# Fused attention and two MLPs on one core: raw weights of the key stage in batch 0's buffers, first attention ahead of a step's narrowing, last weight splits two blocks apart

## The chip, the cores and the metric

The kernel runs on one core of a Trainium2 chip. The metric is the device time of one execution in microseconds (us), as the median of three runs. The engines are called PE (TensorE, matrix multiplication), DVE (VectorE), ACT (ScalarE) and POOL (GpSimd); SP issues the DMAs.

## The reference

The weights of the two MLPs arrive as float64; the kernel reads them as pairs of 32-bit integers ("wide" weights) and makes float32 of them itself, which is called narrowing here. The reference, cut to what matters:

```python
def sm_attn(qq, kk, vv):                  # softmax attention, scale 1/sqrt(64)
    ...
p_packed = sm_attn(p, k, v)               # 32 packed rows per head read k and v
out = sm_attn(q, p_packed, p_packed)      # 576 rows per head read the packed rows
x = out.transpose(0, 2, 1, 3).reshape(4608, 512)      # 8 batches x 576 rows, 8 heads x 64
xn = x / sqrt(mean(x * x) + 1e-6) * rms_g
x = (silu(xn @ w_gate) * (xn @ w_val)) @ w_out        # 512 -> 1536 -> 512
h = x @ moe2_w_in                                     # 512 -> 2048
return (h * cos(h)) @ moe2_w_out                      # 2048 -> 512
```

## The kernel before

A float32 product is made of three matmuls (`mm3`, L151 to L153): each operand is split into a high and a low part (`hilo`, high on ACT, L101, low on DVE or POOL, L102).

**Key stage** (about the first 178 us). Its loop runs over 18 steps; step i deals with one pair of batch and half of the heads, 16 pairs in all. A step loads one or two raw weights (`w_load`, 512 KB each, 20 over the stage: 16 of w_gate and w_val, 4 of w_out), loads K for step i+4, stores finished tiles, then does on PE the transposes of the previous exponentials (`u_et`, tile et), its own scores (`u_s1`, L391, 16 matmuls into s) and the transposes of the next K (`u_prep`, `u_kt`, tiles pt and kp); DVE takes the maximum over the scores (L395, mx), ACT the exponential. Then `u_pp` multiplies with V into pp (result cd on DVE, L433). Between these stand other pieces of work:

- Narrowing of the raw weight that was loaded one step before: part a on ACT (L129), part b on DVE, four operations (L137, L140, L143, L146) that end in the tile wy or, for w_out, ny. A w_out weight is split besides (wohl).
- Attention of batch 0 (`attend(0)`), cut into parts by the words of `ATT_ORD0`; `bg0_step(i, n)` takes the next n parts. x parts multiply, ACT squares and DVE adds into ssq (L295); r sums ssq on PE (rp, L301) and DVE makes ri of it (L303); s scales the attention rows by it (L312); p transposes them (atp) and splits the result (apt), which the projection reads. One part is taken ahead of `u_pp`, two more (one from step 15 on) at the end of the step. 34 parts belong to the key stage.
- `unit(0, u)`: the weights of batch 0, multiplied out on PE (mps) and split into wmhl.

The order is written by hand: each engine runs its instructions in the order of the code, and SP issues all DMAs in that order too. Raw weights lie in five places of the pool u3 (tag wraw).

**Projection stage**: 8 batches of 24 blocks; a block is 12 matmuls gv, silu (ACT L677, DVE L678 and L679), the split shl, and 12 matmuls acc. Its first steps in batch 0 load, narrow and split the weights that remain (wy 16 to 23, w_out 4 to 11; `wy_prep`, `WO_AT`) in a pool wo1 of eight places that is opened when the key stage is over.

**Last stage**: 144 blocks hp (12 matmuls), kk, r, |r|, sine and product (`h_block`, L876 to L883), and the output matmuls ops. Its first weights are read back in float32 (wmraw), and split (wmhl) on ACT and POOL by `wm_split`. A scheduler sets the order of this stage.

Of the kernel before, what the change touches and what calls it, by code (L numbers as in the profile page):

```python
# [20 lines left out]
def kernel(  # L21
# [14 lines left out]
    nc = tc.nc  # L36
# [39 lines left out]
    WO_AT = {4: (-1, 0), 5: (1, 3), 6: (3, 6), 7: (6, 9), 8: (9, 11), 9: (10, 13), 10: (13, 15), 11: (14, 17)}  # L76
# [103 lines left out]
    gT = u1.tile([128, H], F32, name="gT")  # L180
# [149 lines left out]
    def load_k(i):  # L330
# [3 lines left out]
        pn = u3.tile([128, 2, D], F32, tag="pn", name="pn", bufs=3)  # L334
# [23 lines left out]
    load_v(2)  # L358

    def u_prep(i):  # L360
# [4 lines left out]
        nc.vector.tensor_copy(pT[i % 2][:, :, :NP], pt.rearrange("p (h n) -> p h n", h=4))  # L365
        z["kT"], z["kn"] = u4.tile([128, 4, HALF], F32, tag="kT", name="kT"), kn
# [17 lines left out]
    def u_s1(i):  # L384
# [3 lines left out]
        pz = pT[i % 2].rearrange("p h x -> p (h x)")  # L388
# [160 lines left out]
    def wm_split(pool=wm_p):  # L549
# [27 lines left out]
    for i in range(NG + 2):  # L577
# [38 lines left out]
        load_v(i + 3)  # L616
        bg0_step(i, 0 if i == U_ATT else 2 if i < 15 else 1)
# [7 lines left out]
    wo_p = [wo_p[0], ctx.enter_context(tc.tile_pool(name="wo1", bufs=NF1 - WO_U, reuse_waits="tile"))]  # L625
# [225 lines left out]
    while wm_q:  # L851
        wm_split()
# [112 lines left out]
```

## Time and profile before

| | us |
|---|---|
| median of 3 runs | 1755.45 (1754.77 to 1756.66) |
| profiled execution | 1762.2 |
| its span in the profile | 1760.4 |
| PE busy in the span | 1685.1 (96%) |
| DVE busy | 1119.1 (64%) |
| ACT busy | 835.2 (47%) |
| POOL busy | 68.7 (4%) |
| DMA queue of SP | 163.62 MB, 30.5% of the span |

Times in the profile count from the start of the span. Steps of the key stage can be told by their first score matmul: step 0 begins at 8.75 us, step 7 at 71.21, step 8 at 82.73, step 10 at 103.59, step 13 at 132.08 and step 14 at 146.61; the first gv of the projection is at 177.60.

### The profile page before, as it was taken

The numbers are of one execution on the slowest core, as the hardware profiler recorded it, in microseconds if no ns is written. First come the engines' busy times: TensorE is split into PE (matmuls) and PEld (weight loads), VectorE is DVE, ScalarE is ACT, GpSimd is POOL, SyncE is SP. The second block draws the span as 40 slices with busy tenths as digits, with TensorE's granted clock in tenths as the row PEclk, the third lists the DMA queues.
The fourth block names the chain that finished last, engine by engine and source line by source line (L and its number), as shares of the span: only waits on it lengthen the run. The fifth ranks groups of instructions, "written<-read, shape, count | busy, mean of one in ns | idle before, by whom it ended". The sixth has DMA issues, their size and how long they took to land.

```text
span 1760.4 us, 28289 instructions
## 1 busy us (share of the span) xinstructions
PE 1685.1 (96%) x11184; PEld 1463.1 (83%) x11184; DVE 1119.1 (64%) x2180; ACT 835.2 (47%) x1597; POOL 68.7 (4%) x66
## 2 busy tenths in 40 slices
PE   6776889999999999999999999999999999999998
PEld 5554778999999898999999788888888888888887
DVE  2566787677777686866556755555555656565554
ACT  3454443444444444444445654555455545455453
POOL 0000321000000000000002100000000000000000
PEclk9888899999999999999999999999999999999999
DMA  9993732345352534442234200000000000000000
GB/s 232 263 249 117 225 134 94 125 145 182 110 194 92 179 121 161 137 138 76 86 104 139 86 22 27 24 25 24 25 24 25 24 25 25 25 1 25 0 25 24
DMA packets 90564, 165.42 MB, mean 94 GB/s; under 512 B 26432, under 2 KB 48960, under 8 KB 90432
## 3 DMA queue, kind: packets, MB, share of 16 engines
q1 hardware_dynamic: 90432, 163.62, 30.5%
q8 instruction: 88, 1.44, 0.3%
q14 instruction: 44, 0.36, 0.1%
HBM read 128.45 MB, written 35.13 MB: 93 GB/s over the span
## 4 chain that ended last, share of the span: by engine, by line
PE 83%; DVE 6%; DMA 6%; ACT 3%; issue 1%; SPq 0%; POOL 0%; DVEq 0%; ACTq 0%
PE ops L153 7%; PE ops L151 7%; PE ops L152 7%; PE hp L151 7%; PE hp L152 7%; PE hp L153 7%; PE gv L151 5%; PE acc L151 5%; PE acc L152 5%; PE acc L153 5%; PE gv L152 5%; PE gv L153 5%; PE mps L523 3%; PE sp L234 2%; DMA kn<-in_k_dram 1%; PE s L391 1%
## 5 line engine op out<-in xcount | busy, mean ns | idle before, releaser
L151 PE MATMUL gv<-apt,wmhl 128*128 128x288 f32 x768 | 237.8, 310 | 7.7 <-DVE silu L678 6.3
L151 PE MATMUL acc<-shl,wohl 128*128 128x288 f32 x768 | 235.3, 306 | 6.2 <-ACT x L711 5.7
L152 PE MATMUL acc<-shl,wohl 128*128 128x288 f32 x768 | 229.1, 298 | 0.0
L153 PE MATMUL acc<-shl,wohl 128*128 128x288 f32 x768 | 228.8, 298 | 0.0
L152 PE MATMUL gv<-apt,wmhl 128*128 128x288 f32 x768 | 227.6, 296 | 0.0
L151 PE MATMUL hp<-xhl,wmhl 128*128 128x512 f32 x576 | 224.8, 390 | 2.3 <-DVE r L883 2.3
L153 PE MATMUL gv<-apt,wmhl 128*128 128x288 f32 x768 | 226.7, 295 | 0.0
L152 PE MATMUL hp<-xhl,wmhl 128*128 128x512 f32 x576 | 224.8, 390 | 0.0
L153 PE MATMUL hp<-xhl,wmhl 128*128 128x512 f32 x576 | 224.7, 390 | 0.0
L151 PE MATMUL ops<-w2hl,ghl 128*128 128x512 f32 x576 | 224.2, 389 | 0.0
L152 PE MATMUL ops<-w2hl,ghl 128*128 128x512 f32 x576 | 224.1, 389 | 0.0
L153 PE MATMUL ops<-w2hl,ghl 128*128 128x512 f32 x576 | 222.7, 389 | 0.0
L883 DVE TENSOR_TENSOR r<-r,hp 128x512 f32<-128x512 f32 x144 | 99.1, 688 | 185.3 <-ACT r L882 185.3
L881 ACT ACTIVATE r<-r 128x512 f32<-128x512 f32 x144 | 91.1, 633 | 244.8 <-DVE r L880 244.7
L101 ACT ACTIVATE shl<-silu 128x288 fp32r<-128x288 f32 x192 | 85.4, 445 | 235.6 <-DVE silu L679 233.6
L151 PEld LDWEIGHTS gv<-apt,wmhl 128*128 128x128 f32 x768 | 145.0, 189 | 50.0 <-DVE silu L678 9.6
L876 ACT ACTIVATE kk<-hp,magic 128x512 f32<-128x512 f32 x144 | 99.3, 690 | 125.3 <-PE hp L153 125.2
L151 PEld LDWEIGHTS acc<-shl,wohl 128*128 128x128 f32 x768 | 145.8, 190 | 6.8 <-ACT x L711 6.0
L152 PEld LDWEIGHTS acc<-shl,wohl 128*128 128x128 f32 x768 | 146.1, 190 | 0.0
L152 PEld LDWEIGHTS gv<-apt,wmhl 128*128 128x128 f32 x768 | 145.5, 189 | 0.0
L153 PEld LDWEIGHTS acc<-shl,wohl 128*128 128x128 f32 x768 | 145.4, 189 | 0.0
L153 PEld LDWEIGHTS gv<-apt,wmhl 128*128 128x128 f32 x768 | 145.2, 189 | 0.0
(131 smaller groups left out, 2965.6 us busy)
## 6 DMA issues: line engine op xcount, KB each, us to landing
wy<-wy SPq DMA_DIRECT2D x96, 512.0 KB, 4.3
kn<-in_k_dram SPq DMA_DIRECT2D x16, 576.0 KB, 6.5
vn<-in_v_dram SPq DMA_DIRECT2D x48, 192.0 KB, 5.8
qnat<-in_q_dram SPq DMA_DIRECT2D x32, 288.0 KB, 5.1
x_dram<-x SPq DMA_DIRECT2D x32, 288.0 KB, 2.8
x1raw<-x_dram SPq DMA_DIRECT2D x18, 512.0 KB, 4.0
raw<-in_moe_w_in_dram SPq DMA_DIRECT2D x16, 512.0 KB, 5.8
raw<-in_moe_w_out_dram SPq DMA_DIRECT2D x16, 512.0 KB, 5.2
```

Of the source, the lines that this page charges most:

```text
L101: nc.scalar.activation(out=hi, in_=src, func=AF.Copy)
L151: nc.tensor.matmul(ps, lhi, rhi, start=first, stop=False)
L152: nc.tensor.matmul(ps, lhi, rlo, start=False, stop=False)
L153: nc.tensor.matmul(ps, llo, rhi, start=False, stop=last)
L234: nc.tensor.matmul(sp[:, i, 2 * c:2 * c + 2, :], qT[:, i, c * CP:(c + 1) * CP], bq[:, 2 * j + i], start=True, stop=True,)
L391: nc.tensor.matmul(s1[:, r, :HALF], pz[rows, h * 128:(h + 1) * 128], kT[rows, h], start=h == 0, stop=h == 3)
L523: nc.tensor.matmul(ps[kt][h * NP:(h + 1) * NP], ppT[b // 4][rows, 4 * kt + h, n:n + NP], w_y[2 * u + kt][rows, j], start=True, stop=True,)
L876: nc.scalar.activation(out=kk, in_=hp, func=AF.Identity, scale=1.0 / TWO_PI, bias=magic[:, 0:1])
L881: nc.scalar.activation(out=r, in_=r, func=AF.Abs)
L883: nc.vector.tensor_tensor(out=r, in0=r, in1=hp, op=ALU.mult)
```

## The change

1. The pool wo1 is opened ahead of the key stage, and the stage's raw weights use its eight places (tag wo; in the order they read as wo where they read wraw before). The pools u3 and u4 go; V has three places instead of four, pn four instead of three, pT one tile instead of two.
2. The 20 raw weights come in steps 1 to 15 instead of 1 to 16, two at steps 3, 6, 9, 12 and 15 (before: 4, 8, 12 and 16). Two weights are so narrowed in steps 4, 7, 10, 13 and 16 (before: 5, 9, 13 and 17).
3. Four raw weights of batch 0 (wy 16, 17, 18 and w_out 4) are loaded in steps 15 to 17 (`B0_L`); the rest is loaded three ahead instead of two, and w_out 4 is narrowed one block later.
4. V is loaded at the end of step i for step i+2 instead of i+3, and one V load ahead of the stage goes.
5. The second call of `bg0_step` stands ahead of part b of the narrowing and always takes two parts, so the 34th is taken in step 16 and not in step 17.
6. In the passage to the last stage two weight items are split on DVE instead of POOL, at blocks 3 and 5, the next two are loaded there, and the loads and splits of the next x rows come two blocks (the second split one block) later.

```diff
-    WRAW_B = 5
...
-    W_FROM, W_TO = 1, 17
+    W_FROM, W_TO = 1, 16
...
+    B0_L = {15: (16,), 16: (17, -4), 17: (18,)}
...
-    WO_AT = {4: (-1, 0), 5: (1, 3), 6: (3, 6), 7: (6, 9), 8: (9, 11), 9: (10, 13), 10: (13, 15), 11: (14, 17)}
+    WO_AT = {4: (-1, 1), 5: (0, 3), 6: (3, 6), 7: (6, 9), 8: (9, 11), 9: (10, 13), 10: (13, 15), 11: (14, 17)}
...
-    wo_p = [ctx.enter_context(tc.tile_pool(name="wo0", bufs=WO_U))]
+    wo_p = [ctx.enter_context(tc.tile_pool(name=f"wo{x}", bufs=(WO_U, NF1 - WO_U)[x])) for x in range(2)]
...
-    u3 = ust.enter_context(tc.tile_pool(name="u3", bufs=2))
-    u4 = ust.enter_context(tc.tile_pool(name="u4", bufs=1))
-    u5 = ust.enter_context(tc.tile_pool(name="u5", bufs=2))
...
-    pT = [u1.tile([128, 4, 160], F32, name=f"pT{i}") for i in range(2)]
-    for t in pT:
-        nc.gpsimd.memset(t, 0.0)
+    pT = u1.tile([128, 4, 160], F32, name="pT")
+    nc.gpsimd.memset(pT, 0.0)
...
-        pn = u3.tile([128, 2, D], F32, tag="pn", name="pn", bufs=3)
+        pn = u2.tile([128, 2, D], F32, tag="pn", name="pn", bufs=4)
...
-        vn = nat_v[i] = u2.tile([CP, 4, NC_, D], F32, tag="vn", name="vn", bufs=4)
+        vn = nat_v[i] = u2.tile([CP, 4, NC_, D], F32, tag="vn", name="vn", bufs=3)
...
-    load_v(2)
...
-        w_raw[n] = load_w(pool, tag, w[r:r + 128, c * 512:(c + 1) * 512], bufs, kt == 1)
+        w_raw[n] = load_w(wo_p[1], "wo", w[r:r + 128, c * 512:(c + 1) * 512], swap=kt == 1)
...
-        wo_raw[f] = load_w(pool, tag, w_out[f * 128:(f + 1) * 128, :], {"wraw": WRAW_B}.get(tag))
+        wo_raw[f] = load_w(wo_p[1], "wo", w_out[f * 128:(f + 1) * 128, :])
...
-    def wm_split(pool=wm_p):
+    def wm_split(pool=wm_p, eng=None):
...
-            hilo(raw[:, :, a * 128:(a + 1) * 128], t[:, 0], t[:, 1], (nc.vector, nc.gpsimd)[pool is wm_p])
+            hilo(raw[:, :, a * 128:(a + 1) * 128], t[:, 0], t[:, 1], eng or nc.gpsimd)
...
         load_k(i + 4)
+        for n in B0_L.get(i, ()):
+            (wy_load if n >= 0 else wo_load)(abs(n))
...
             unit(0, U_S[i])
+        bg0_step(i, 0 if i == U_ATT else 2)
         for n in w_q:
             w_prep(n, 1)
         for n in wo_q:
             wo_split(n - W_KV, 1)
         wo_q = [n for n in w_q if n >= W_KV]
         w_q = due
-        load_v(i + 3)
-        bg0_step(i, 0 if i == U_ATT else 2 if i < 15 else 1)
+        load_v(i + 2)
...
-    wo_p = [wo_p[0], ctx.enter_context(tc.tile_pool(name="wo1", bufs=NF1 - WO_U, reuse_waits="tile"))]
...
-    for n in range(W_B0, W_B0 + 2):
-        wy_load(n, wo_p[1], "wo")
-    wo_load(WO_U, wo_p[1], "wo")
     for _ in bg0:
         pass
     att_load(1)
...
-            if n + 2 < 4 * NCK:
-                wy_load(n + 2, wo_p[1], "wo")
+            if n + 3 < 4 * NCK:
+                wy_load(n + 3)
...
-    while wm_q:
-        wm_split()
...
+            late_x = 2 * (n == 0)
+            if f == 10 + late_x and n + 1 < NCH:
                 load_x(n + 1)
-            if f in (12, 14) and n + 1 < NCH:
-                split_x(n + 1, f // 14)
-            if n == 0 and f in (3, 4):
-                wm_load(("w", NCK + f - 3))
-            if n == 0 and f in (9, 11):
-                wm_split(b4)
+            if f in (12 + late_x, 14 + late_x // 2) and n + 1 < NCH:
+                split_x(n + 1, f // (14 + late_x // 2))
+            if n == 0 and f in (3, 5, 9, 11):
+                wm_split(wm_p if f < 6 else b4, nc.vector)
+            if n == 0 and f in (3, 5):
+                wm_load(("w", NCK + f // 4))
```

What becomes of the order, at three places. DVE in step 13 of the key stage, before (from the last squares of batch 0's attention, ssq, to ri):

```order
L295 TENSOR_TENSOR ssq<-ssq,sq 128x288
L433 TENSOR_SCALAR cd<-pp,mx 128x128
L137 TENSOR_SCALAR wy<-wy 128x512
L140 TENSOR_SCALAR wy<-wy 128x512
L143 SCALAR_TENSOR_TENSOR wy<-wraw,wy 128x512
L146 SCALAR_TENSOR_TENSOR wy<-wraw,wy 128x512
L137 TENSOR_SCALAR wy<-wy 128x512
L140 TENSOR_SCALAR wy<-wy 128x512
L143 SCALAR_TENSOR_TENSOR wy<-wraw,wy 128x512
L146 SCALAR_TENSOR_TENSOR wy<-wraw,wy 128x512
L295 TENSOR_TENSOR ssq<-ssq,sq 128x288
L303 TENSOR_SCALAR ri<-rp 96x3
```

and now:

```order
L292 TENSOR_TENSOR ssq<-ssq,sq 128x288
L429 TENSOR_SCALAR cd<-pp,mx 128x128
L292 TENSOR_TENSOR ssq<-ssq,sq 128x288
L300 TENSOR_SCALAR ri<-rp 96x3
L137 TENSOR_SCALAR wy<-wy 128x512
L140 TENSOR_SCALAR wy<-wy 128x512
L143 SCALAR_TENSOR_TENSOR wy<-wo,wy 128x512
L146 SCALAR_TENSOR_TENSOR wy<-wo,wy 128x512
L137 TENSOR_SCALAR ny<-ny 128x512
L140 TENSOR_SCALAR ny<-ny 128x512
L143 SCALAR_TENSOR_TENSOR ny<-wo,ny 128x512
L146 SCALAR_TENSOR_TENSOR ny<-wo,ny 128x512
```

The second ssq and ri have moved from behind eight narrowing operations (L137 to L146) to ahead of them; the second weight narrowed there is one of w_out (ny).

SP at the end of the key stage, before (stores of the stage at L536, then the raw weights of batch 0, then bq and bdf for the attention of batch 1):

```order
L536 DMA q_79<-tf 128x128
L536 DMA c_71<-cd 128x64
L536 DMA wy_86<-wy 128x1024
L536 DMA q_79<-tf 128x128
L536 DMA wy_87<-wy 128x1024
L115 DMA wo<-in_moe_w_gate_dram 128x1024 x2
L115 DMA wo<-in_moe_w_out_dram 128x1024
L211 DMA bq<-q_73 64x8x32 x2
L214 DMA bdf<-c_65 32x2x64 x4
L112 DMA wo<-in_moe_w_gate_dram 64x1024
```

and now:

```order
L115 DMA wo<-in_moe_w_gate_dram 128x1024
L115 DMA wo<-in_moe_w_out_dram 128x1024
L532 DMA q_78<-tf 128x128
L532 DMA c_71<-cd 128x64
L532 DMA wy_86<-wy 128x1024
L112 DMA wo<-in_moe_w_gate_dram 64x1024
L113 DMA wo<-in_moe_w_gate_dram 64x1024
L532 DMA q_79<-tf 128x128
L532 DMA c_71<-cd 128x64
L532 DMA wy_87<-wy 128x1024
L532 DMA q_79<-tf 128x128
L208 DMA bq<-q_73 64x8x32 x2
```

The raw weights of w_gate and w_out (the loads with 512 KB or its halves into wo) now stand ahead of the last stores; bq directly follows the stores.

ACT at the end of the projection stage and the start of the last one, before (silu and shl belong to the last projection blocks, kk to the last stage's first blocks, x to the projection's results):

```order
L677 ACTIVATE silu<-gv_11700 128x288
L101 ACTIVATE shl<-silu 128x288
L101 ACTIVATE w2hl<-w2raw 128x512
L677 ACTIVATE silu<-gv_11740 128x288
L101 ACTIVATE shl<-silu 128x288
L101 ACTIVATE w2hl<-w2raw 128x512 x2
L876 ACTIVATE kk<-hp,magic 128x512
L711 ACTIVATE x_11805<-acc 128x288
L711 ACTIVATE x_11809<-acc 128x288
L101 ACTIVATE w2hl<-w2raw 128x512
L101 ACTIVATE wmhl<-wmraw 128x512 x4
L876 ACTIVATE kk<-hp,magic 128x512
```

and now:

```order
L101 ACTIVATE wmhl<-wmraw 128x512 x2
L101 ACTIVATE shl<-silu 128x288
L101 ACTIVATE w2hl<-w2raw 128x512
L674 ACTIVATE silu<-gv_11730 128x288
L101 ACTIVATE wmhl<-wmraw 128x512 x2
L101 ACTIVATE shl<-silu 128x288
L101 ACTIVATE w2hl<-w2raw 128x512 x2
L868 ACTIVATE kk<-hp,magic 128x512 x2
L708 ACTIVATE x_11795<-acc 128x288
L708 ACTIVATE x_11799<-acc 128x288
L101 ACTIVATE w2hl<-w2raw 128x512
L101 ACTIVATE wmhl<-wmraw 128x512 x4
```

Two pairs of wmhl copies stand between silu and shl of the last projection blocks now, two kk instead of one ahead of the x copies, and the four wmhl copies behind w2hl are those of the next two items.

## Rows read from the trace of the kernel before

**Rows 1.** Page, part 4: chain that ended last, shares of the span.

```profile
PE 83%; DVE 6%; DMA 6%; ACT 3%; issue 1%; SPq 0%; POOL 0%; DVEq 0%; ACTq 0%
```

**Rows 2.** Windows: length, busy PE, PEld, DVE, ACT, POOL (count), PEclk, DMA share, GB/s.

```profile
80.00:100.00 20.00, 16.79 (x142) 12.47 (x146) 8.36 (x22) 7.10 (x18) 0.00 (x0) 0.74 1.00 256
...
146.00:150.00 4.00, 4.00 (x21) 2.55 (x20) 0.00 (x0) 0.97 (x2) 0.54 (x1) 0.62 0.45 132
...
200.00:220.00 20.00, 17.53 (x137) 16.22 (x136) 18.29 (x33) 10.18 (x24) 9.55 (x7) 0.91 0.78 229
...
980.00:1740.00 760.00, 759.05 (x3342) 628.36 (x3343) 452.12 (x740) 386.11 (x599) 0.02 (x1) 1.00 0.08 23
```

**Rows 3.** Page, part 6: DMA issues, count, KB each, median us to landing.

```profile
vn<-in_v_dram SPq DMA_DIRECT2D x48, 192.0 KB, 5.8
...
x_dram<-x SPq DMA_DIRECT2D x32, 288.0 KB, 2.8
```

**Rows 4.** Waits of PE from 20 to 200 us: total us, times, longest.

```profile
PE qtp L224 <- DMA qnat<-in_q_dram: 3.3, 2, 1.7
PE atp L266 <- DVE mx L418: 2.7, 1, 2.7
```

**Rows 5.** Timeline of DVE in steps 13 and 14: start, us, operation, xcount [idle before].

```profile
139.19 0.42 DVE L137 TENSOR_SCALAR wy<-wy 128x512 f32<-128x512 f32 x1
...
143.69 0.45 DVE L295 TENSOR_TENSOR ssq<-ssq,sq 128x288 f32<-128x288 f32 x1
...
150.06 0.76 DVE L395 TENSOR_REDUCE mx<-s 128x1 f32<-128x576 f32 x1 [4.28 <-PE s L391]
```

**Rows 6.** Timeline of PE: step 10, then steps 13 and 14.

```profile
102.84 0.82 PE L415 MATMUL et<-ident,e 128*96 128x128 f32 x6
103.59 2.21 PE L391 MATMUL s<-kT,pT 64*128 64x288 f32 x16
...
144.20 1.12 PE L301 MATMUL rp<-ones,ssq 128*96 128x1 f32 x6 [6.33 <-DVE ssq L295]
145.19 1.50 PE L415 MATMUL et<-ident,e 128*96 128x128 f32 x6
146.61 3.40 PE L391 MATMUL s<-kT,pT 64*128 64x288 f32 x16
```

**Rows 7.** Timeline of DVE in step 10.

```profile
107.83 0.74 DVE L395 TENSOR_REDUCE mx<-s 128x1 f32<-128x576 f32 x1
```

**Rows 8.** Timeline of ACT in step 13.

```profile
139.11 0.41 ACT L294 ACTIVATE sq<-xp 128x288 f32<-128x288 f32 x1 [0.59 <-DVE ssq L295]
```

**Rows 9.** Timeline of PE at the end of the key stage.

```profile
176.47 1.43 PE L266 MATMUL atp<-ident,s 96*128 96x96 f32 x6 [3.95 <-DVE s L312]
177.60 0.59 PE L151 MATMUL gv<-apt,wmhl 128*128 128x288 f32 x1
```

**Rows 10.** Timeline of ACT in batch 0's first blocks.

```profile
184.83 0.66 ACT L129 ACTIVATE ny<-wo 128x512 f32<-128x512 f32 x1 [2.48 <-DMA wo<-in_moe_w_out_dram]
```

**Rows 11.** Timeline of DVE in batch 0's first blocks.

```profile
185.82 0.45 DVE L678 TENSOR_TENSOR silu<-silu,gv 128x288 f32<-128x288 f32 x1 [3.73 <-ACT silu L677]
```

**Rows 12.** Timeline of ACT where the last stage begins.

```profile
973.21 2.18 ACT L101 ACTIVATE wmhl<-wmraw 128x512 fp32r<-128x512 f32 x4
975.30 0.68 ACT L876 ACTIVATE kk<-hp,magic 128x512 f32<-128x512 f32 x1
...
978.39 0.72 ACT L882 ACTIVATE r<-r,halfpi 128x512 f32<-128x512 f32 x1
```

**Rows 13.** Timeline of SP where the last stage begins.

```profile
972.00 1.19 SPq L713 DMA_DIRECT2D x_dram<-x  x2
```

**Rows 14.** Timeline of DVE where the last stage begins.

```profile
980.23 0.68 DVE L883 TENSOR_TENSOR r<-r,hp 128x512 f32<-128x512 f32 x1
```

**Rows 15.** Timeline of PE where the last stage begins.

```profile
980.95 0.50 PE L151 MATMUL hp<-xhl,wmhl 128*128 128x512 f32 x1 [2.26 <-DVE r L883]
...
982.04 0.63 PE L152 MATMUL hp<-xhl,wmhl 128*128 128x512 f32 x1
```

More of the change, by code (lines that the diff above doesn't have):

```diff
@@ L168 @@
     psb = [ps_bg]
-    wo_p = [ctx.enter_context(tc.tile_pool(name="wo0", bufs=WO_U))]
+    wo_p = [ctx.enter_context(tc.tile_pool(name=f"wo{x}", bufs=(WO_U, NF1 - WO_U)[x])) for x in range(2)]
     ust = ExitStack()
+    u5 = ust.enter_context(tc.tile_pool(name="u5", bufs=4))
+    u2 = ust.enter_context(tc.tile_pool(name="u2", bufs=2))
     u1 = ust.enter_context(tc.tile_pool(name="u1", bufs=1))
-    u2 = ust.enter_context(tc.tile_pool(name="u2", bufs=2))
-    u3 = ust.enter_context(tc.tile_pool(name="u3", bufs=2))
-    u4 = ust.enter_context(tc.tile_pool(name="u4", bufs=1))
-    u5 = ust.enter_context(tc.tile_pool(name="u5", bufs=2))
     ps_2 = pst.enter_context(tc.tile_pool(name="ps_2", bufs=KP_B, space=PSUM))
@@ L179 @@
     top, bot = slice(0, 64), slice(64, 128)
-    gT = u1.tile([128, H], F32, name="gT")
+    gT = const.tile([128, H], F32, name="gT")
     ppT = [pp_p.tile([128, H, 128], F32, tag=f"pp{i}", name=f"ppT{i}") for i in range(B // 4)]
-    pT = [u1.tile([128, 4, 160], F32, name=f"pT{i}") for i in range(2)]
-    for t in pT:
-        nc.gpsimd.memset(t, 0.0)
+    pT = u1.tile([128, 4, 160], F32, name="pT")
+    nc.gpsimd.memset(pT, 0.0)
     bq = a1.tile([128, H, 2 * NP], F32, name="bq")
@@ L364, in u_prep @@
         nc.tensor.transpose(pt, pn.rearrange("p a d -> p (a d)"), ident)
-        nc.vector.tensor_copy(pT[i % 2][:, :, :NP], pt.rearrange("p (h n) -> p h n", h=4))
-        z["kT"], z["kn"] = u4.tile([128, 4, HALF], F32, tag="kT", name="kT"), kn
+        nc.vector.tensor_copy(pT[:, :, :NP], pt.rearrange("p (h n) -> p h n", h=4))
+        z["kT"], z["kn"] = u1.tile([128, 4, HALF], F32, tag="kT", name="kT"), kn
     def u_kt(i, ms):
@@ L387, in u_s1 @@
         s1 = ps_1.tile([128, 2, 512], F32, tag="s1", name="s1")
-        pz = pT[i % 2].rearrange("p h x -> p (h x)")
+        pz = pT.rearrange("p h x -> p (h x)")
         for h in range(4):
@@ L458, in w_load, with wy_load @@
         if n >= W_KV:
-            wo_load(n - W_KV, u3, "wraw")
+            wo_load(n - W_KV)
             return
-        wy_load(n, u3, "wraw", WRAW_B)
-    def wy_load(n, pool, tag, bufs=None):
+        wy_load(n)
+    def wy_load(n):
         t, j = divmod(n, 2)
@@ L468, in wy_load @@
         r = (2 * kt + j) * 128
-        w_raw[n] = load_w(pool, tag, w[r:r + 128, c * 512:(c + 1) * 512], bufs, kt == 1)
+        w_raw[n] = load_w(wo_p[1], "wo", w[r:r + 128, c * 512:(c + 1) * 512], swap=kt == 1)
     def w_prep(n, part):
         if n >= W_KV:
-            wo_prep(n - W_KV, u3, part)
+            wo_prep(n - W_KV, u1, part)
             return
@@ L495, with wo_load @@
     wo_y = {}
-    def wo_load(f, pool, tag):
-        wo_raw[f] = load_w(pool, tag, w_out[f * 128:(f + 1) * 128, :], {"wraw": WRAW_B}.get(tag))
+    def wo_load(f):
+        wo_raw[f] = load_w(wo_p[1], "wo", w_out[f * 128:(f + 1) * 128, :])
     def wo_prep(f, pool, part):
@@ L828 @@
             wy_prep(n, 0)
-            if n + 2 < 4 * NCK:
-                wy_load(n + 2, wo_p[1], "wo")
+            if n + 3 < 4 * NCK:
+                wy_load(n + 3)
         for n, (at, to) in WO_AT.items():
             if at == i:
-                wo_load(n, *((wo_p[1], "wo")))
+                wo_load(n)
             if to == i:
```

1 line of the change is left out of this document (removed).

## Prediction

> **What bounds the kernel now.** I read the chain of work that ended last first [rows 1]: 83% of it is TensorE, and DVE and DMA have 6% each. The windows say where those 12% lie: from 980 us to 1740 us TensorE is busy for 759.05 of 760.00 us, but in the first 260 us it is not [rows 2]. From 80 to 100 us the DMA engines are the full resource (share 1.00, 256 GB/s, TensorE busy 16.79 of 20); from 200 to 220 us it is DVE (18.29 of 20). So nothing that the change does behind 260 us can gain much, with one exception: the stall in the passage to the last stage, at 980 us. I then went through TensorE's waits in the first stage, the key stage, and asked at each which input came last.
>
> The profiled execution took 1762.2 us, 1.8 over its span and 6.7 over the median of the three runs (1755.45). The terms below are differences of that execution; I carry their sum to the median unchanged. About 0.2% (3.5 us) is what a measurement of this kernel can tell from no change.
>
> **Part 1, the loads of the key stage.** One V load, of three parts of 192.0 KB [rows 3], leaves the prologue, and each later V load is issued one step later. So up to step 9 every raw weight stands 576 KB earlier in SP's queue, while one raw weight more (20 loads over 15 steps and not 16) comes ahead of the later ones, and the q loads now stand ahead of their step's V. For a q load of steps 7 and 8 that is 576 + 576 - 512 = 640 KB less ahead of it. At 256 GB/s it lands 2.5 us earlier. It is on the path: TensorE waited for q for 3.3 us in two waits [rows 4]. What the earlier steps gain on their raw weights flows through the same stream of bytes into these two waits, so I don't add it. Term: **-2.5 us**; bounds 0 (the second raw weight, which comes one step sooner, takes it back) and -3.3 (both q waits gone). V one step later costs nothing: it is issued at the end of step i and used in step i+3, two whole steps later, and lands 5.8 us after its issue [rows 3]; if that cover were gone, each step would wait up to 576 KB at 256 GB/s, 2.3 us. Eight places for raw weights instead of five, one pT instead of two and fewer V places release nothing that the trace shows waited for, and the copy into pT already stood behind the scores that read it: nothing, either way.
>
> **Part 2, which steps narrow two weights.** Narrowing one weight costs DVE half of the 4.50 us from 139.19 to 143.69, 2.25 us [rows 5]. The steps with two of them were 5, 9, 13 and 17 and become 4, 7, 10, 13 and 16. Step 9's pair stands ahead of step 10's maximum: the scores ended at 103.59 + 2.21 = 105.80 [rows 6], and the maximum over them, which all that follows waits for, started at 107.83 [rows 7], so up to 2.03 us could come back. At step 10 the opposite: DVE's row there becomes 2.25 us longer, and TensorE already waited 2.7 us behind it, for L418 early in step 11 [rows 4]. I take a gain of 0.5 there, since the scores themselves come earlier by part 1 while DVE's work does not, and a loss of 1.4 at step 10, since some of the 2.25 is met by the shorter step before. Term: **+0.9 us**; bounds -2.0 and +2.25.
>
> **Part 3, attention ahead of the narrowing.** In step 13 the matmuls rp start at 144.20 after a wait of 6.33 us for DVE's sum of squares ssq [rows 6]. ScalarE had done the square at 139.11 + 0.41 = 139.52 [rows 8]; DVE first did cd and two narrowings, 139.19 to 143.69, and only then ssq [rows 5]. In the changed order ssq stands ahead of both narrowings. It can start at 139.55 and end near 140.05, so rp starts at 140.1 and not 144.2. The two narrowings come behind ri, which waits for rp (140.1 + 1.12), and so end near 141.4 + 4.5 = 145.9, beside the transposes et and the scores; the next maximum, now at 150.06 after 4.28 us of DVE idle [rows 5], is wanted 4.1 earlier, at 146.0. The cover is just enough. Term: **-4.1 us**; bounds -2.0 (DVE arrives 2 us later at this point, by part 2) and -6.0 (with the clock, rival B).
>
> Behind that wait the granted clock was 0.62 from 146 to 150 us [rows 2], mostly the lower of its two levels (1.2 of 2.4 GHz), and et and the scores ran slowly. The Trainium skill has the rule for it (TensorE: Matmul & The Clock Gate, Part 1: The HAM clock gate): the array's clock is 1.2 GHz after idleness and 2.4 GHz under work, and the trace agrees. By that rule a short enough wait would leave the clock up, and the sum would be rival B's.
>
> **Part 4, the end of the key stage.** DVE did the last two narrowings ahead of s, TensorE's transposes atp waited 3.95 us for that until 176.47, and gv, the first matmul of the projection, started at 177.60 [rows 9]. The third part of attention per step puts ssq, rp and s one step earlier, ahead of these narrowings. DVE's work is the same, though: the last pair now stands ahead of the apt copies that gv needs, and so most of the 3.95 returns there. Term: **-0.7 us**; bounds 0 and -3.9. Key stage together: -2.5 + 0.9 - 4.1 - 0.7 = -6.4, gv at about 171.2.
>
> **Part 5, batch 0's first raw weights.** Four of them are now issued in steps 15 to 17 instead of after the stage. ScalarE, at 184.83, waited 2.48 us for the first w_out weight, and the silu behind it kept DVE idle for 3.73 us until 185.82 [rows 10, 11]. Both go: the weight has landed, and its narrowing stands one block later. Of the 3.73 I keep 0.66, the length of one such ScalarE operation [rows 10], since another one may stand in its place: 3.1 us. From there DVE is the full resource to about 240 us (200 to 220 us: 18.29 of 20), with the same number of operations, so the gain holds. Term: **-3.1 us**; bounds -1.0 and -3.7.
>
> **Part 6, the passage to the last stage.** Two of the items that POOL subtracted go to DVE, into the last two projection blocks; TensorE has two blocks in hand there, so this costs nothing, or up to the 2.26 us of the stall below if that cover is gone. The next four ScalarE copies, wmhl, started at 973.21; now they write where the tiles of the last x stores lay, so they wait until these land: issued from 972.00 over 1.19 us, landing 2.8 us after the issue, which is 976.0 and, with 0.7 of allowance, 976.7 [rows 3, 12, 13]. That is 3.5 us later. The sine at the end of ScalarE's row ended at 978.39 + 0.72 = 979.11, but its product r*hp started on DVE only at 980.23 [rows 12, 14], so 1.1 of it is met, and one kk (0.68) moves from behind the copies to ahead of them: 3.5 - 1.1 - 0.7 = 1.7, and 0.3 for the slower clock behind a longer stall. TensorE waited 2.26 us for that product, until 980.95 [rows 15]. Term: **+2.0 us**; bounds -2.3 (the stall gone: POOL no longer works beside DVE) and +4.0 (nothing of the 3.5 met, and a slower clock behind it: the matmul at 980.95 took 0.50, that at 982.04 took 0.63).
>
> **Sum:** -2.5 + 0.9 - 4.1 - 0.7 - 3.1 + 2.0 = -7.5. The profiled time would be 1754.7, the median 1755.45 - 7.5 = **1748.0 us**.
>
> **Rivals.**
> A. *DVE takes the key stage's gain back.* The pairs at steps 4, 7, 10, 13 and 16 stand directly ahead of the next maximum. If each costs its step what the reordering gains, gv stays at 177.60 and only parts 5 and 6 are left: -3.1 + 2.0 = -1.1, 1754.4 us. For it: five pairs and not four, and the wait of 2.7 us of step 11. Against it: the 4.28 us of DVE idle behind step 13's pair, which this rival would have to fill.
>
> B. *The clock stays up.* Behind the 6.33 us wait et took 1.50 and the scores 3.40; at full clock they took 0.82 and 2.21 [rows 6]: 1.87 us per step that is spared the lower level. With the waits of step 13 and of the end shortened that may happen twice, and with the stall of part 6 gone besides: -7.5 - 3.7 - 2.0 = -13.2, about 1742 us, and 1743 to 1745 with part of it. Against it: the wait left in step 13 is still about 2.2 us, and in this trace a wait of 2.26 was enough for the fall behind it, to 0.63 at 982.04 [rows 15]. So it is not in the sum.
>
> C. *Slower: the steps behind the new pair fall to the lower clock.* Step 10 runs its scores at full clock now. If the pair at step 10 makes TensorE wait in each of the steps 10 to 16, each loses 1.87 us: seven steps give +13.1 and 1748.0 + 13.1 = 1761 us. It decides from the sixth such step on, since -7.5 + 6 x 1.87 = +3.7 is the first to pass 3.5. For it: scores take both 2.21 and 3.40 in this stretch, so the steps lie close to that edge. Against it: step 14 is at the lower level already and has nothing to lose, and part 3 removes waits.
>
> That the change doesn't do what it says is ruled out as far as order goes: in the instruction order the narrowings do stand behind ssq and s.
>
> **How the numbers follow.** Forecast (parts 1 to 6 near their values) 0.62; A 0.16; B 0.13; C 0.09. Faster by over 0.2% (below 1751.9) are the forecast and B: 0.75. Within 0.2% is A: 0.16. Slower is C: 0.09. Range: the bounds of parts 3, 4 and 6 give about 4 us to either side of 1748; down to 1740 it takes in B, up to 1755.5 it takes in A. What stays out is C and the ends where several bounds meet.
>
> **What the changed profile would show.** Right: rp's wait for ssq in step 13 near 2 us instead of 6.33; the two waits for q together under 1 us; gv at about 171; no ScalarE wait for w_out in batch 0; r*hp about 2 us later relative to the last x copies. Wrong: the maximum of steps 8, 11 and 14 late behind narrowings with TensorE idle ahead of et (A); scores of steps 10 to 15 all at 3.4 us (C); scores of step 14 at 2.2 us (B). The forecast falls if gv comes later than 174 us or the stall ahead of 985 us passes 6 us.

## The result: slower, 1767.3 us, and the time is lost where the change was not meant to act

The changed kernel takes 1767.32 us (median of 4 runs, 1766.38 to 1768.69) against 1755.67 us (4 runs): a ratio of 1.0067, 95% interval 1.0049 to 1.0084, or 11.7 us more. Its profiled execution took 1766.95 us, with a span of 1765.2. The forecast was 7.5 us less.

The first views say that the loss isn't where the change is. Windows of the kernel after (length, busy PE, PEld, DVE, ACT and POOL with counts, PEclk, DMA share, GB/s):

```profile
80.00:100.00 20.00, 18.39 (x273) 14.05 (x278) 12.33 (x31) 10.85 (x27) 0.00 (x0) 0.97 1.04 288
...
200.00:220.00 20.00, 16.22 (x122) 13.73 (x121) 18.80 (x32) 11.40 (x20) 8.79 (x6) 1.00 0.35 120
...
980.00:1740.00 760.00, 760.00 (x3291) 617.34 (x3290) 436.68 (x716) 373.29 (x579) 0.00 (x0) 1.00 0.07 20
```

From 980 to 1740 us TensorE is busy all the time, nearly as it was before (759.05 us), and at full clock (1.00). But 3291 matmuls fall into these 760 us; before it was 3342 [rows 2]. A busy share cannot show that. The distances from one matmul's start to the next do. Timeline of PE in the kernel after, in the last stage (start, us, operation):

```profile
1103.01 0.40 PE L151 MATMUL hp<-xhl,wmhl 128*128 128x512 f32 x1
1103.24 0.40 PE L152 MATMUL hp<-xhl,wmhl 128*128 128x512 f32 x1
1103.48 0.40 PE L153 MATMUL hp<-xhl,wmhl 128*128 128x512 f32 x1
1103.71 0.40 PE L151 MATMUL hp<-xhl,wmhl 128*128 128x512 f32 x1
...
1105.58 0.40 PE L153 MATMUL hp<-xhl,wmhl 128*128 128x512 f32 x1
1105.81 0.39 PE L151 MATMUL ops<-w2hl,ghl 128*128 128x512 f32 x1
1106.04 0.40 PE L152 MATMUL ops<-w2hl,ghl 128*128 128x512 f32 x1
...
1107.88 0.39 PE L151 MATMUL ops<-w2hl,ghl 128*128 128x512 f32 x1
1108.10 0.39 PE L152 MATMUL ops<-w2hl,ghl 128*128 128x512 f32 x1
```

The same in the kernel before:

```profile
1101.01 0.39 PE L151 MATMUL hp<-xhl,wmhl 128*128 128x512 f32 x1
1101.23 0.39 PE L152 MATMUL hp<-xhl,wmhl 128*128 128x512 f32 x1
1101.46 0.39 PE L153 MATMUL hp<-xhl,wmhl 128*128 128x512 f32 x1
...
1102.14 0.39 PE L153 MATMUL hp<-xhl,wmhl 128*128 128x512 f32 x1
1102.37 0.39 PE L151 MATMUL ops<-w2hl,ghl 128*128 128x512 f32 x1
1102.59 0.39 PE L152 MATMUL ops<-w2hl,ghl 128*128 128x512 f32 x1
```

Before, one matmul follows another every 226.7 ns (mean over the starts from 1000 to 1740 us), without exception. After, it takes 233.4 ns on average from one hp to the next and 228.9 from one ops to the next: the first five of an ops group of twelve are slow (228 to 235 ns, means by place in the group), the last seven are at 226.7. With 1728 of each kind that is 1728 x 6.7 + 1728 x 2.2 = 15.4 us.

Where the two profiled executions stand, from the starts in the timelines:

| | before, us | after, us | difference |
|---|---|---|---|
| step 9 begins | 93.8 | 87.1 | -6.7 |
| step 9 to step 13 | 38.3 | 37.5 | -0.8 |
| step 13 to step 14 | 14.5 | 10.4 | -4.1 |
| step 14 to step 15 | 10.9 | 11.0 | +0.1 |
| step 15 to the first gv | 20.1 | 20.9 | +0.8 |
| first gv to the 145th | 67.3 | 66.0 | -1.3 |
| 145th gv to the last | 717.7 | 717.0 | -0.7 |
| last gv to the last ops | 792.7 | 810.5 | +17.8 |

At the last gv the changed kernel is 12.8 us ahead, more than was forecast for that place. Everything, and more, goes behind it. The order of the instructions there differs only in the first few blocks, so the first question is what else the change touched.

### The profile page after: what moved, and what is told of

Read it like the earlier page. It is cut to its first block, busy times and chain, and to the rows that moved or that the text cites. A ratio compares the mean times of both kernels' runs of the same rounds, so it can differ in the third digit from the quotient of the medians.

```text
span 1765.2 us, 28275 instructions
## 1 busy us (share of the span) xinstructions
PE 1691.8 (96%) x11184; PEld 1456.1 (82%) x11184; DVE 1118.9 (63%) x2184; ACT 833.2 (47%) x1597; POOL 61.6 (3%) x61
## 4 chain that ended last, share of the span: by engine, by line
PE 82%; DVE 6%; DMA 5%; ACT 3%; issue 3%; SPq 1%; POOL 1%; DVEq 0%; ACTq 0%; POOLq 0%
PE hp L151 8%; PE hp L152 8%; PE hp L153 8%; PE ops L151 7%; PE ops L152 7%; PE ops L153 7%; PE gv L151 5%; PE acc L151 5%; PE acc L152 5%; PE acc L153 5%; PE gv L152 5%; PE gv L153 5%; PE mps L519 2%; PE sp L231 1%; DMA wo<-in_moe_w_val_dram 1%
## 5 line engine op out<-in xcount | busy, mean ns | idle before, releaser
L151 PE MATMUL gv<-apt,wmhl 128*128 128x288 f32 x768 | 237.4, 309 | 10.9 <-DVE silu L675 7.6
L151 PE MATMUL hp<-xhl,wmhl 128*128 128x512 f32 x576 | 229.2, 398 | 3.8 <-DVE r L875 3.8
L152 PE MATMUL hp<-xhl,wmhl 128*128 128x512 f32 x576 | 228.9, 397 | 0.0
L153 PE MATMUL hp<-xhl,wmhl 128*128 128x512 f32 x576 | 228.6, 397 | 0.0
L151 PEld LDWEIGHTS gv<-apt,wmhl 128*128 128x128 f32 x768 | 144.8, 188 | 52.4 <-DVE silu L675 12.0
L869 DVE TENSOR_SCALAR kk<-kk 128x512 f32<-128x512 f32 x144 | 61.4, 426 | 138.7 <-ACT kk L868 138.5
L152 PEld LDWEIGHTS gv<-apt,wmhl 128*128 128x128 f32 x768 | 145.0, 189 | 0.0
```

Of the source, the lines that this page charges most:

```text
L151: nc.tensor.matmul(ps, lhi, rhi, start=first, stop=False)
L152: nc.tensor.matmul(ps, lhi, rlo, start=False, stop=False)
L153: nc.tensor.matmul(ps, llo, rhi, start=False, stop=last)
L869: nc.vector.tensor_scalar(out=kk, in0=kk, scalar1=-MAGIC, scalar2=None, op0=ALU.add)
```

## Experiments

### Is it the place of the tiles?

One line of the change seemed to have no cost at all. Neither the diff ahead of the prediction nor the prediction has it: gT, 32 bytes in each partition, moved from the pool u1 to const. SBUF, the memory that the engines work on, is filled from two sides here: most pools are laid one after another from the low addresses up (the left side), some from the high addresses down (the right side). const is the lowest pool, and so every left tile of the last stage starts 32 bytes higher in the compiled program (wmhl from 33504 to 33536, ghl from 158432 to 158464). xhl lies on the right side, at 196576, and doesn't move.

**a_gt_u1**

```diff
-    gT = const.tile([128, H], F32, name="gT")
+    gT = u1.tile([128, H], F32, name="gT")
```

> The changed kernel with one line undone: the tile gT (32 bytes per partition) is taken from the pool u1 again and not from const, so every tile on the left side of SBUF lies 32 bytes lower, as in the kernel before. In the changed kernel's trace the key stage and batch 0 are 12.8 us ahead of before at the last gv, the passage to the last stage gives back about 4, and then each matmul of the last stage starts some 232 to 235 ns after the one before it instead of 226.7, which costs 13.7 us over 3456 matmuls. Theory P (place in SBUF): the matmul interval depends on where its operands lie; here it is 226.7 ns throughout, and the time is 1767.3 - 13.7 = about 1753.5 us. Rival O (order: DVE instead of POOL splits, later x loads, another phase of ACT and DVE against PE in the last stage): interval and time stay as in the changed kernel, about 1767 us.

Measured: 1754.71 us (10 runs), ratio to before 0.9997 (0.9983 to 1.0012). The interval is 226.7 ns for hp and ops, and from the last gv to the last ops it takes 794.8 us instead of 810.5. Its window in the last stage:

```profile
1000.00:1200.00 200.00, 200.00 (x884) 165.62 (x883) 116.46 (x191) 100.68 (x156) 0.00 (x0) 1.00 0.08 22
```

**b_gt_const**

```diff
-    gT = u1.tile([128, H], F32, name="gT")
+    gT = const.tile([128, H], F32, name="gT")
```

> The kernel before with that one line alone: gT in const, all left tiles 32 bytes higher, nothing else of the change. Theory P: the last stage's interval goes from 226.7 ns to 232 to 235 ns and the time from 1755.7 to about 1769 us. Rival O: 1755.7 us, interval unchanged.

Measured: 1771.69 us (4 runs), ratio 1.0093 (1.0068 to 1.0118); hp 233.4 ns, ops 228.9, as in the changed kernel.

```profile
1000.00:1200.00 200.00, 200.00 (x867) 162.57 (x866) 115.15 (x188) 98.21 (x153) 0.00 (x0) 1.00 0.07 22
```

The two together settle the cause of the loss: this one line makes the kernel before slower by 16 us, and without it the change is no slower than before. Rival O (the order) has fallen. Why the place of a tile costs time is another question; the runs that follow ask which place counts.

**a_pad32**

```diff
     magic = const.tile([128, 1], F32, name="magic")
+    pad = const.tile([128, 8], F32, name="pad")
+    nc.gpsimd.memset(pad, 0.0)
```

> The changed kernel with another unused tile of 32 bytes in const, so that the left tiles lie 64 bytes above those of the kernel before. Theory P with a period of 64 bytes: fast again, about 1753.5 us. Theory P with a longer period or with the distance to xhl (which does not move) as the cause: slow, 1760 to 1767 us, or another interval. Rival O: 1767 us.

Measured: 1769.84 us (5 runs), ratio 1.0072 (1.0047 to 1.0097); hp 233.4, ops 228.7 ns. A period of 64 bytes is out.

**a_right32**

```diff
+    rp_p = ctx.enter_context(tc.tile_pool(name="rp", bufs=1, side="right"))
+    nc.gpsimd.memset(rp_p.tile([128, 8], F32, name="pad"), 0.0)
     ast = ExitStack()
```

> The changed kernel with an unused tile of 32 bytes at the right end of SBUF, so that xhl (the moving operand of hp) lies 32 bytes lower and stands to wmhl as in the kernel before, modulo 64, while all left tiles stay where the changed kernel has them. If the places of moving and stationary operand relative to each other count: hp back at 226.7 ns, about 1757 us, ops unchanged. If the stationary tile's own place counts: hp stays at 232 to 235 ns, 1767 us. If the moving tile's own place counts: hp was slow for another reason and changes either way.

Measured: 1767.24 us (4 runs), ratio 1.0066 (1.0044 to 1.0088); hp 233.4, ops 228.7 ns. It is slow, so the case that I had worked out for a period of 64 doesn't hold. But the sequence of intervals, 233 and 234 ns in turn, is the one of a_pad32 and not that of the changed kernel (235 and 232). In both, xhl and wmhl are 64 bytes nearer to each other than before. That pointed to the distance with a longer period.

**b_gt_right96**: b_gt_const with the tile of a_right32 at 24 elements (96 bytes).

> The kernel before with gT in const (left tiles 32 bytes higher) and an unused tile of 96 bytes at the right end (xhl 96 bytes lower): all tiles now start at a multiple of 128 bytes, and the distance between wmhl and xhl is again a multiple of 128. Theory R (the distance between the operand that streams and the weights that are loaded meanwhile counts, with a period of 128 bytes or less): the last stage's interval is 226.7 ns for hp and ops, time about 1756 us. Theory L (the left tile's own place counts: only 96 modulo 128 was fast so far): 233 ns, about 1769 us. If the period is longer than 128 it is slow as well.

Measured: 1771.9 us (one run); hp 232.8, ops 228.4 ns, with a third pattern (in hp 237.5 and 229 ns in turn, but 224 for the second of a group). Slow: a period of 128 is out, and this run alone could not tell a longer period from theory L.

```profile
1000.00:1200.00 200.00, 200.00 (x870) 162.91 (x868) 114.63 (x187) 98.19 (x152) 0.00 (x0) 1.00 0.08 22
```

**b_pad128**: the kernel before with the tile of a_pad32 at 32 elements (128 bytes).

> The kernel before with an unused tile of 128 bytes in const: left tiles 128 bytes higher, at 96 modulo 128 as in the kernel before, xhl unmoved. Theory L (the left tile's own place, modulo 128): 226.7 ns, about 1756 us. Theory R256 (the distance of xhl to wmhl counts, with a period of 256 bytes; in the kernel before the distance is a multiple of 256, in b_gt_right96 an odd multiple of 128): another, slow interval, about 1770 us, with the same pattern as b_gt_right96 (229, 237, 238 and 224 ns).

Measured: 1767.07 us (one run); hp 232.8, ops 228.4 ns, with the pattern of b_gt_right96. Theory L has fallen.

**b_gt_right224**: b_gt_const with the right tile at 56 elements (224 bytes).

> The kernel before with gT in const (left tiles 32 bytes higher, at 0 modulo 128) and an unused tile of 224 bytes at the right end, so that xhl moves down by 224 and the distance to wmhl shrinks by 256 bytes. Theory R256: 226.7 ns, about 1756 us. Theory L: 233 ns, about 1770 us.

Measured: 1754.28 us (one run); hp and ops 226.7 ns, as a period of 256 bytes has it.

```profile
1000.00:1200.00 200.00, 200.00 (x885) 165.58 (x884) 116.88 (x192) 100.48 (x156) 0.00 (x0) 1.00 0.08 22
```

Of the seven layouts of tiles in SBUF, those with the same distance from wmhl (its lowest tile) to xhl have the same intervals, to 0.1 ns in hp, whichever side was moved:

| kernel | wmhl at | xhl at | distance modulo 256 | hp, ns | ops, ns |
|---|---|---|---|---|---|
| before, a_gt_u1 | 33504 | 196576 | 0 | 226.7 | 226.7 |
| b_gt_right224 | 33536 | 196352 | 0 | 226.7 | 226.7 |
| after, b_gt_const | 33536 | 196576 | 224 | 233.4 | 228.9 |
| a_pad32 | 33568 | 196576 | 192 | 233.4 | 228.7 |
| a_right32 | 33536 | 196544 | 192 | 233.4 | 228.7 |
| b_gt_right96 | 33536 | 196480 | 128 | 232.8 | 228.4 |
| b_pad128 | 33632 | 196576 | 128 | 232.8 | 228.4 |

(The other wmhl tiles of the last stage lie a multiple of 256 bytes further on, and the second xhl tile does too.)

### The parts of the change

**b_att_first**

```diff
             unit(0, U_S[i])
+        bg0_step(i, 0 if i == U_ATT else 2)
         for n in w_q:
             w_prep(n, 1)
...
-        bg0_step(i, 0 if i == U_ATT else 2 if i < 15 else 1)
```

> The kernel before with part 5 of the change alone: the second call of bg0_step stands ahead of part b of the narrowing and always takes two parts. By the prediction: rp's wait of 6.3 us in step 13 falls to about 2.2, so that step 13 to step 14 takes 10.4 and not 14.5 us, the end of the key stage gives or takes under 1 us, and step 9 to the first gv takes about 79.7 and not 83.7 us: 1755.7 - 4 = about 1752 us. Rival (DVE gives it back at the next maximum): 83.7 us and 1755.7.

Measured: 1755.3 us (10 runs), ratio 0.9987 (0.9971 to 1.0003): no clear difference. rp's wait did fall, and step 13 to step 14 took 10.9 us. But step 15 to the first gv took 23.1 us instead of 20.1 to 20.8. Timeline of PE in b_att_first, step 13 and the end of the key stage:

```profile
135.42 1.12 PE L301 MATMUL rp<-ones,ssq 128*96 128x1 f32 x6 [2.47 <-DVE ssq L295]
...
161.18 0.67 PE L301 MATMUL rp<-ones,ssq 128*96 128x1 f32 x6 [2.82 <-DVE ssq L295]
166.39 2.18 PE L266 MATMUL atp<-ident,s 96*128 96x96 f32 x12 [4.38 <-DVE ppT L448]
171.90 0.61 PE L151 MATMUL gv<-apt,wmhl 128*128 128x288 f32 x1 [3.33 <-DVE apt L102]
```

With the loads of the kernel before, three narrowings stand between s and apt at the end, and gv waits for them. In the changed kernel, with the loads one step earlier (W_TO), two narrowings stand there, and the same stretch takes 20.9 us. So the gain in step 13 alone says little on the time. Some time also went ahead of step 13: step 9 to step 13 took 40.3 us in this execution and 36.9 to 38.3 in the five others with the old loads; the scores of step 9 took 3.90 us here and 2.21 in b_gt_const. Whether the order has a part in that is not shown.

**a_gt_oldB**: a_gt_u1 with the passage to the last stage as in the kernel before.

```diff
...
-            late_x = 2 * (n == 0)
-            if f == 10 + late_x and n + 1 < NCH:
+            if f == 10 and n + 1 < NCH:
...
-            if n == 0 and f in (3, 5, 9, 11):
-                wm_split(wm_p if f < 6 else b4, nc.vector)
...
+            if n == 0 and f in (9, 11):
+                wm_split(b4)
```

> The changed kernel with gT in u1 and the passage to the last stage as in the kernel before (two items split by POOL, loads at blocks 3 and 4). By the prediction's part 6 the changed passage costs 2.0 us: from the last gv to the last output matmul 794.8 us in a_gt_u1, here 792.7 as in the kernel before; time 1754.7 - 2 = about 1752.7 us. Rival (the passage costs nothing): 794.8 and 1754.7.

Measured: 1753.23 us (10 runs), ratio 0.9976 (0.9957 to 0.9995); from the last gv to the end 792.7 us against 794.8 in a_gt_u1. TensorE's waits at the passage, in a_gt_oldB (line waited for, total us, times, longest):

```profile
PE hp L151 <- DVE r L877: 2.3, 1, 2.3
```

The changed passage costs 2.1 us between these marks. Part 6 of the prediction holds. The total times (1753.23 and 1754.71, with overlapping intervals) can't show 2 us.

**a_gt_wo4**: a_gt_u1 with w_out 4 narrowed from block 0 on, as in the kernel before.

```diff
-    WO_AT = {4: (-1, 1), 5: (0, 3), ...
+    WO_AT = {4: (-1, 0), 5: (0, 3), ...
```

> The changed kernel with gT in u1, and w_out 4 narrowed from block 0 on as in the kernel before (w_out 5 stays at block 3). In the changed kernel ScalarE waits 2.8 us in batch 0 until POOL has read ny for the split of w_out 4, because w_out 5 goes into the same single tile one block later; the silu behind it is 3.5 us later than the blocks ahead had won. Theory N: this wait is what takes part 5's gain back; without it the first 144 gv matmuls take about 63 us instead of 66.1, and the time is 1754.7 - 2.5 = about 1752 us. Rival (DVE is full there in any case): 66 us and 1754.7.

Measured: the first 144 gv take 63.05 us instead of 66.08, and ScalarE's wait for POOL is gone from its waits (170 to 205 us, a_gt_wo4):

```profile
ACT shl L101 <- DVE silu L676: 13.8, 6, 4.5
ACT qT L225 <- PE qtp L221: 1.0, 1, 1.0
ACT wmhl L101 <- PE mps L519: 0.2, 1, 0.2
```

So the wait was what took part 5's gain back in this stretch. The time did not follow: 1755.28 us (10 runs), a ratio of 0.9988 (0.9975 to 1.0001), where 1752 was expected and a_gt_u1 has 1754.71. The runs of these two kernels spread over 6 and 10 us, their intervals overlap, and the profiled execution came to step 9 1.6 us later than that of a_gt_u1; so the 3 us are shown in the stretch and not in the time.

**a_gt_late**: a_gt_u1 with part b of the last two narrowings behind the loop's end and the apt copies.

```diff
...
-        for n in w_q:
+        for n in w_q if i < W_TO else ():
             w_prep(n, 1)
...
+        w_l = w_q if i == W_TO else w_l
         w_q = due
...
     for _ in bg0:
         pass
+    for n in w_l:
+        w_prep(n, 1)
```

> The changed kernel with gT in u1 and the last two narrowings' part b behind the copies apt, nothing else. If the 6.6 us wait at the end of the key stage is these two narrowings: step 15 to the first gv 16.5 us instead of 20.9; the time falls by what batch 0 doesn't take back, 1 to 4 us, to about 1752. Rival: the wait stays (ppT is late for another reason), 1754.7.

Measured: 1752.95 us (10 runs), ratio 0.9975 (0.9959 to 0.9991). Step 15 to the first gv takes 16.3 us instead of 20.9, and the first 144 gv take 67.8 instead of 66.1: 2.9 of 4.6 us stay. Timeline of PE at the end of the key stage, a_gt_late; the 6.62 us wait for ppT is now 2.12:

```profile
162.80 2.18 PE L263 MATMUL atp<-ident,s 96*128 96x96 f32 x12 [2.12 <-DVE ppT L444]
164.69 0.59 PE L151 MATMUL gv<-apt,wmhl 128*128 128x288 f32 x1
```

**a_best**: gT in u1, w_out 4 from block 0, the old passage and the late narrowing together.

> The changed kernel with four corrections: gT in u1 (place), w_out 4 narrowed from block 0 on, the passage to the last stage as in the kernel before, and part b of the key stage's last two narrowings behind the copies apt instead of ahead of them. From the profiles so far: 226.7 ns in the last stage; first 144 gv matmuls 63 us; last gv to end 792.7 us; and the wait of TensorE for ppT behind the two narrowings at the end of the key stage, 6.6 us in the changed kernel, falls by up to 4.5, so that step 15 to the first gv takes about 16.5 instead of 20.9 us (some of it comes back, since DVE does the same work in batch 0). Against a_gt_u1 (1754.7): -3.0 - 2.1 - 2 to -4.5, about 1747 us, ratio to before about 0.995. Rival (DVE is full in batch 0 and takes all of the last gain back): about 1750 us.

Measured: **1746.99 us** (6 runs, 1744.20 to 1751.14), ratio 0.9948 (0.9935 to 0.9961): it beats both kernels. Step 15 to gv 16.4 us, last gv to the end 792.7 us, 226.7 ns. The first 144 gv take 67.3 us, not 63: with the late narrowing in batch 0, DVE is what bounds these blocks, and the gain of a_gt_wo4 shrinks to 0.5 us. That the time is near the forecast of 1748.0 us is chance: the late narrowing was not in the forecast, and the cost of the passage, which was, is not in this kernel. Its windows:

```profile
204.00:214.00 10.00, 9.41 (x70) 9.20 (x70) 9.65 (x18) 8.53 (x13) 4.76 (x3) 1.00 0.44 159
214.00:224.00 10.00, 3.71 (x22) 3.24 (x21) 9.59 (x19) 3.17 (x8) 1.78 (x2) 0.81 0.24 73
```

## Why the prediction was wrong, by its steps

The step that failed stands ahead of the sum: nothing that the change does behind 260 us can gain much, since TensorE is busy there, with the passage as the one exception. This asked only what could be gained. A loss behind the passage was put at nothing without a reason, and a full engine can still become slower per instruction. The sum has no term for where the tiles lie, and it is 15.7 us (810.46 - 794.77, after against a_gt_u1; the medians of the two lie only 12.6 us apart, and in the profiled executions the changed kernel was 3.3 us ahead at the last gv). None of the rivals contained it either. Rival C's 1761 us was slower by another mechanism, which did not occur: in the changed kernel the scores of steps 10, 11 and 13 still took 2.21 us. Nor could the two conditions under which the forecast was to fall have shown it. They look at times ahead of 985 us, and neither came true: gv came at 166.88 us and not behind 174, and the stall took 3.75 us and not 6.

The other terms, each with what the trace of after showed. Where several profiles have the same code in a stretch, the mean is given.

**Part 1, loads (-2.5).** Not settled. The start of step 9 lies between 86.6 and 94.5 us over the six profiles that have the loads of the kernel before (mean 90.5), and between 86.6 and 92.6 over the eight that have the new ones (mean 89.4). The difference of 1.1 us is no more than the scatter; one execution's 93.8 us for the kernel before was near the slow end, and its 3.3 us over that mean are about half of the 6.7 by which it exceeded the median. The q waits that I took as the measure did not go: they are one wait of 3.5 us instead of two with 3.3 [rows 4]. PE's waits of after:

```profile
PE qtp L221 <- DMA qnat<-in_q_dram: 3.5, 1, 3.5
```

**Part 2, pairs of narrowings (+0.9).** Step 9 to step 13 takes 37.5 us in five profiles with the old code and 37.5 in eight with the new: 0.0.

**Part 3, ssq ahead of the narrowings (-4.1).** Right to 0.1 us: 14.52 to 10.37. The rows that answer to [rows 5, 6, 8], PE and then DVE of after:

```profile
132.58 1.12 PE L298 MATMUL rp<-ones,ssq 128*96 128x1 f32 x6 [2.18 <-DVE ssq L292]
133.56 1.49 PE L411 MATMUL et<-ident,e 128*96 128x128 f32 x6
134.99 4.21 PE L387 MATMUL s<-kT,pT 64*128 64x288 f32 x16
```

```profile
132.07 0.46 DVE L292 TENSOR_TENSOR ssq<-ssq,sq 128x288 f32<-128x288 f32 x1 [0.27 <-ACT sq L291]
...
133.82 0.41 DVE L137 TENSOR_SCALAR wy<-wy 128x512 f32<-128x512 f32 x1
...
137.70 0.69 DVE L146 SCALAR_TENSOR_TENSOR ny<-wo,ny 128x512 int32<-128x512 int32 x1
...
139.25 0.76 DVE L391 TENSOR_REDUCE mx<-s 128x1 f32<-128x576 f32 x1 [0.59 <-PE s L387]
```

The wait is 2.18 us where I had written "about 2.2". DVE, done with the narrowings, was idle for 0.59 us before the next maximum could start: the cover was just enough, and with some luck. The scores took 0.81 us longer than before; had they not, the maximum would have been some 0.2 us late (an estimate from these rows). Rival A fell here. So did B: behind the 2.18 us the granted clock was 0.50, the lower level of 1.2 GHz, from 135 to 139 us, and the scores took 4.21 us (3.40 before).

```profile
135.00:139.00 4.00, 4.00 (x17) 2.54 (x16) 3.48 (x8) 0.49 (x1) 0.00 (x0) 0.50 0.92 302
```

**Part 4, the end of the key stage (-0.7).** Step 15 to the first gv takes 20.5 us with the old code (five profiles) and 20.9 with the new (six): +0.4. The mechanism was the one told, the last pair ahead of the apt copies. It also stands ahead of ppT, and takes a little more than all of the 3.95 us [rows 9]:

```profile
164.99 2.18 PE L263 MATMUL atp<-ident,s 96*128 96x96 f32 x12 [6.62 <-DVE ppT L444]
166.88 0.59 PE L151 MATMUL gv<-apt,wmhl 128*128 128x288 f32 x1
```

a_gt_late shows what my sum left lying there: 2.9 us.

**Part 5, batch 0's raw weights (-3.1).** The DMA wait [rows 10] did go, and the silu of block 1 came 2.57 us behind that of block 0 (171.50 - 168.93) where it was 5.73 in the timeline of before (185.39 - 179.66). What I had not asked is where w_out 4's later narrowing puts the next one. There is one tile ny, and w_out 5 needs it at block 3, when POOL has just begun to read it for the split of w_out 4. ACT of after:

```profile
168.93 0.41 ACT L674 ACTIVATE silu<-gv 128x288 f32<-128x288 f32 x1
...
171.50 0.38 ACT L674 ACTIVATE silu<-gv 128x288 f32<-128x288 f32 x1
...
190.30 0.66 ACT L129 ACTIVATE ny<-wo 128x512 f32<-128x512 f32 x1 [2.81 <-POOL wohl L507]
190.86 0.39 ACT L674 ACTIVATE silu<-gv 128x288 f32<-128x288 f32 x1
```

The 2.48 us wait for a DMA has become a 2.81 us wait for POOL three blocks later. From the first gv to the last it is 783.6 us in the mean of five profiles with the old code (782.6 to 785.1) and 783.6 in five with the new (783.0 to 783.8): the term is 0, to about 1 us. a_gt_wo4 shows that it would have been about -3.0 but for this. The step that failed in this term is the last of its working: with the same number of operations the gain was to hold, and who needs ny next was not asked.

**Part 6, the passage (+2.0).** Right: +2.05 (a_gt_u1 794.77, before 792.72), and by the mechanism told. ACT, DVE and PE of after, against [rows 12, 14, 15]:

```profile
964.22 2.20 ACT L101 ACTIVATE wmhl<-wmraw 128x512 fp32r<-128x512 f32 x4 [1.82 <-DMA x_dram<-x]
```

```profile
969.57 0.69 DVE L875 TENSOR_TENSOR r<-r,hp 128x512 f32<-128x512 f32 x1 [0.65 <-ACT r L874]
```

```profile
970.31 0.80 PE L151 MATMUL hp<-xhl,wmhl 128*128 128x512 f32 x1 [3.75 <-DVE r L875]
```

The copies wait for the x stores to land, and TensorE for 3.75 us instead of 2.26.

Put together: -1.1 (not separable from 0), 0.0, -4.1, +0.4, 0.0, +2.05 and +15.7 make +12.9; measured were 11.7, with an interval of 8.6 to 14.7. Without the last term the sum is -2.8; a_gt_u1 measured -0.5 by its ratio (-3.0 to +2.1). So even the parts that I had priced gave at most about a third of the 7.5 us that I forecast, because parts 1 and 5 gave little or nothing.

## What to carry to other kernels

When a diff moves a tile from one pool to another, write down which other tiles shift in SBUF by it, and after the run compare the starts of successive matmuls in a stretch that the change should not touch: a busy share of 100% hides a matmul that has become 3% longer. Before forecasting from one profile, see how that execution stands to the median, and in which stretch it differs; here half of the difference lay in the very stretch that was to gain. And when an edit moves an operation on a tile that has one place, look at who needs the tile next.

## What the runs showed of the hardware

For the float32 matmuls hp (128x512) of this kernel, the time from start to start depends on where the streaming operand, xhl, lies in SBUF relative to the left tiles, the weights wmhl among them: 226.7 ns when xhl and wmhl are a multiple of 256 bytes apart, 232.8 to 233.4 ns in each of the three other distances tried (224, 192 and 128 modulo 256). Neither operand's own address counts: b_gt_right224 moved both and is fast, and pairs of kernels with the same distance agree. The gv matmuls of 128x288 are no test of it. They take 133 ns (median, 300 to 950 us) in both kernels, but both of their operands, apt and wmhl, lie on the left and never moved against each other.

The cost is there at full clock only, as far as the traces go. Behind the stall of the passage the granted clock of the changed kernel is 0.50 (971 to 974 us), and hp starts every 426 or 427 ns there, ten times in a row, as it does before (seven times from 982.04 us):

```profile
971.33 0.63 PE L153 MATMUL hp<-xhl,wmhl 128*128 128x512 f32 x1
971.76 0.63 PE L151 MATMUL hp<-xhl,wmhl 128*128 128x512 f32 x1
972.18 0.63 PE L152 MATMUL hp<-xhl,wmhl 128*128 128x512 f32 x1
```

In the timeline the weights of the next matmul are loaded while the present one streams. Timeline of PEld, the weight loads, in the kernel after; the matmuls that start at 1103.01 and 1103.24 are shown further up:

```profile
1103.01 0.19 PEld L152 LDWEIGHTS hp<-xhl,wmhl 128*128 128x128 f32 x1
1103.25 0.19 PEld L153 LDWEIGHTS hp<-xhl,wmhl 128*128 128x128 f32 x1
```

So both operands are read at the same time. That the two reads hinder each other is the nearest explanation, but it is argued and not shown: in every run all left tiles of the last stage moved together, those that DVE and ACT use too, and no run moved wmhl alone. The trace of a_right32 speaks against DVE and ACT: hp's interval is 233.4 ns both while DVE is busy and ACT idle (513 intervals; over 90% and under 10% of the interval) and the other way round (472 intervals). Why the first five matmuls of ops are slow stays open; their operands, w2hl and ghl, lie on the same side, a multiple of 256 bytes apart in all seven layouts. The Trainium skill (SBUF — State Buffer, Who interferes with whom) gives TensorE two read ports, one for the moving operand and one for the weights, and calls them independent, with DVE and GpSimd the only pair that collides. By that rule the 32 bytes would have cost nothing. The measurement differs: they cost 15.7 us, and it decides.

The stretch that is bound by DMA varies by up to 8 us between executions: over the six kernels with the same loads, one profile each, step 9 begins at 86.6 to 94.5 us. Behind it the five of them with the old order vary less: 36.9 to 38.3 us from step 9 to step 13, 14.51 to 14.53 from step 13 to step 14, 782.6 to 785.1 from the first gv to the last.
